# Operand sums of a second-level product: made by transfers inside DRAM instead of on the vector engine

## The chip, the core and the metric

The program runs on one core of a Trainium2 chip. The metric is the device time of one execution in microseconds; the kernel before takes 680.3 us (median of three runs, 679.74 to 681.45).

Engines are named as in the profile: PE is the tensor engine's matmul, PEld its weight load, DVE the vector engine, ACT the scalar engine, POOL the GpSimd engine, SP the sync engine. SP and POOL each issue transfers in their own program order. An instruction that has to wait holds up everything behind it on its engine.

## The reference

`x` is 2048 x 512, float32. The result mixes a Fourier transform and a gated two-layer network with a gate per row:

```
a = x @ dft_hid_re.T ; b = x @ dft_hid_im.T
A = dft_seq_re @ a - dft_seq_im @ b
B = (silu(x @ w1) * (x @ w3)) @ w2          # w1, w3: 512 x 1376
g = sigmoid((x * gate_w).sum(-1))
out = g * A + (1 - g) * B
```

## The kernel before

Every float32 product is made of three matmuls on a split operand: a high part (rounded, made by ACT at line 110) and a low part (the rest, made by DVE at line 113). `mm3` (line 126) issues the three. A matrix product over 2 x 2 blocks is done by a scheme with seven block products instead of eight, so each stage also needs sums of operand blocks; DVE makes those.

**First stage, gate and up projection.** Steps n = 1 to 21 (`gate_up`, line 333) each do seven products of six matmuls on PE. Beside them in a step DVE and ACT combine results (lines 356 to 394), prepare the next weight chunk (`sums_wb`, lines 246 to 249, then a split), and run work that tables attach to a step (`early`, `ahead`, `second`, `mid`, `at_end`, by step number). Line 369 adds PSUM bank `x` to a tile; the seventh product of the same step writes into that bank again, so it waits for line 369.

Three attached jobs matter here. First, steps 2 to 9 (lines 528 to 553) make four sums of quarters of the sequence matrix `cc`: eight 512 KB loads into SBUF on SP's queue (names `q0b`, `q1b`), eight subtractions of 128 x 1024 on DVE (line 546), eight 512 KB stores to a DRAM array `tsp` on POOL's queue (line 547). Their tiles come from the two `ZO` places. Second, four groups of `w2` are loaded, summed, split and stored to `w2sp` (lines 557 to 585), at the steps named in `W2_AT`; the split parts also take the two `ZO` places. Third, the transform's left operands are prepared at the steps in `A1_AT`.

**Second stage, the transform over the sequence.** Blocks 0 to 3 (`KIND` "F"), then two blocks of the down projection ("H") and two of the hidden transform ("Y"). A block is a list of steps; in block 0 a step is twelve matmuls. `step(m)` ends with `advance(m)` (line 762): it asks SP for loads of steps up to m + 8, lets DVE make the operand sum of step m + 4 (lines 730 and 734) and lets ACT and DVE split the operand of step m + 3 (tiles `zo`). `at(blk, n, f)` (line 1206) runs `f` just before step n of a block. In block 0 these are, among others, loads of the second half of the left operand (`load_a2`, tiles `xs`, steps 4 to 11), their subtraction on DVE (line 178, steps 7 to 14) and the gate (`gates`, steps 5 to 8, which ends with two stores on POOL).

**The second level.** Block 2's first product P1 is not done in block 2: it is itself split into seven quarter products m1 to m7, each in two halves "a" and "b", which are set between the steps of blocks 1 and 2 by the table `AMONG` (line 655). m1 uses B11 as it is; m5, m6, m7 and m4 use the quarter sums T1, T2, T3, T4 from `tsp`. m6 adds on to the PSUM bank of m1 after ACT has copied that bank (line 934). The left operands' sums S are made in `sums_s` (line 882).

Nothing reorders the work: each engine runs its instructions in the order in which the program text emits them, and waits on semaphores only for what it needs.

Of the kernel before, what the change touches and what calls it, by code (L numbers as in the profile page):

```python
# [7 lines left out]
F32 = mybir.dt.float32  # L8
F32R = mybir.dt.float32r
AF = mybir.ActivationFunctionType  # L10
ALU = mybir.AluOpType
# [14 lines left out]
LOOK = 3  # L26
K = 9
TAIL = 256
W2_AT = (10, 11, 13, 15)
A1_AT = (12, 14, 16, 17, 18, 19, 20)  # L30


# [1 line left out]
def fnet_swiglu_gate_kernel(  # L34
# [21 lines left out]
    nc = tc.nc  # L56
# [25 lines left out]
    def bank(k, name):  # L82
        return psum.tile([P, 512], F32, tag=f"ps{k}", name=name)
# [8 lines left out]
    def take(places, shape, dtype, name):  # L92
        p, tag = at = places.pop(0)
        t = p.tile(shape, dtype, tag=tag, name=name)
        HELD[id(t)] = t, places, at
        return t
# [4 lines left out]
    def parts(name):  # L101
        return take(ZO, [P, 2, 4, 256], F32R, name)

    def free(*tiles):
        for t in tiles:
            _, places, at = HELD.pop(id(t))
            places.append(at)
# [18 lines left out]
    def mm3(ps, ah, al, bh, bl, first, last, chain=False, some=slice(None)):  # L126
        for n, (u, v) in enumerate(((ah, bh), (ah, bl), (al, bh))):
            matmul(ps, u, v, some, start=first and n == 0, stop=last and n == 2,
                   skip_group_check=chain)
# [11 lines left out]
    tsp = dram.tile([4, 2, P, 1024], F32, tag="tsp", name="tsp")  # L141
# [185 lines left out]
    early, ahead, second, mid, at_end = {}, {}, {}, {}, {}  # L327
# [88 lines left out]
    b12, a21 = zt[0].rearrange("p h a n -> p h (a n)"), zt[1][:, :, 0]  # L416
# [91 lines left out]
    def do(work, n, f, *a):  # L508
        work.setdefault(n, []).append(lambda: f(*a))
# [15 lines left out]
    for n, k in ((7, "B12"), (7, "B11"), (8, "B21"), (9, "B22")):  # L525
        do(early, n, lambda k=k: free(ST[1, k]))

    BQ = {}

    def load_quarter(h, b, t):  # L530
        BQ[h, b] = t
        nc.sync.dma_start(t, cc[2 + (b[2] == "2"), 0, 2 * (b[1] == "2") + h])

    def load_quarters(h):
        for b in ("b11", "b12"), ("b21", "b22"):
            t = BQ[h, b] = parts(f"q{h}{b[0]}")
            v = t.bitcast(F32).rearrange("p h a n -> p h (a n)")
            for i in range(2):
                load_quarter(h, b[i], v[:, i])

    def sum_quarter(h, i):


        to, u, v = (("b11", "b12", "b11"), ("b22", "b22", "b11"),
                    ("b12", "b22", "b12"), ("b21", "b21", "b22"))[i - 1]
        nc.vector.tensor_sub(BQ[h, to], BQ[h, u], BQ[h, v])  # L546
        nc.gpsimd.dma_start(tsp[i - 1, h], BQ[h, to])

    for h, at_n in enumerate(((2, 3, 4, 4, 5), (5, 6, 7, 8, 9))):
        do(at_end, at_n[0], load_quarters, h)  # L550
        for n, i in zip(at_n[1:], (1, 3, 2, 4)):
            do(at_end, n, sum_quarter, h, i)
        do(at_end, at_n[4], lambda h=h: free(BQ[h, ("b11", "b12")], BQ[h, ("b21", "b22")]))

    W2R = {}

    def load_w2(p):
# [47 lines left out]
    for n in range(NI):  # L605
        if n in W2_AT:
            p = W2_AT.index(n)
            do(mid if p > 1 else at_end, n - 1, load_w2, p)
# [3 lines left out]
        if n in A1_AT:  # L612
            p = A1_AT.index(n)
# [9 lines left out]
    n = NI - 1 - LOOK  # L623
    do(at_end, n - 1, F4.extend, [(f4_a, f"f4_{k}") for k in range(4, 5 + LOOK)])
    for k in range(LOOK + 2):
# [26 lines left out]

    QUARTERS = {"m1": ("B11", 0, 0), "m2": ("B11", 0, 1), "m4": ("T4", 1, 1), "m5": ("T1",),
                "m6": ("T2",), "m7": ("T3",), "m3": ("B22",)}
    AMONG = {(1, 22): ("m1a",), (1, 23): ("m1b", "m6a"), (1, 24): ("m6b",), (1, 25): ("m7a",), (1, 26): ("m7b",),
             (1, 27): ("m4a", "m4b"), (2, 4): ("m2a",), (2, 5): ("m2b",), (2, 6): ("m5a",),
             (2, 7): ("m5b",), (2, 8): ("m3a",), (2, 9): ("m3b",)}
    STEPS, NEW, MAT = [], {}, {}
    for blk, nq in enumerate(NQ):
        todo_p1 = []  # L660
        for n, (k, form, q) in enumerate((k, form, q) for k, form in ORDER[blk] for q in range(nq)):
# [7 lines left out]
            STEPS.append((blk, q, k, form))  # L669
            for name in AMONG.get((blk, n), ()):  # L670
                k, h = name[:2], "ab".index(name[2])
# [90 lines left out]
    def advance(m):  # L762
        load_c(m + LEAD + AHEAD)
        sum_c(m + LEAD + 1)
        split_c(m + LEAD)
# [108 lines left out]
    SR, SF, MB = [], {}, {}  # L874
# [7 lines left out]
    def sums_s(j):  # L882
        (a11, a21), (a12, a22) = ((t[:, :, :P], t[:, :, P:]) for t in SR)
        if j == 0:
            nc.vector.tensor_add(a22, a21, a22)
            nc.vector.tensor_sub(a21, a11, a21)
        else:
            nc.vector.tensor_sub(a11, a22, a11)
            nc.vector.tensor_sub(a12, a12, a11)

    def high_s(i):
        SF[i] = [take(F4, [P, 1024], F32R, f"s{i}{k}") for k in "hl"[: 2 - i]]
# [7 lines left out]
    def quarter(k, h, i):  # L900

        kk = 2 * h + i
        if len(QUARTERS[k]) == 3:
            _, r, half = QUARTERS[k]
            w = A1[4 * half + kk][:, :, 1, r * P : (r + 1) * P]
            return w[:, 0], w[:, 1]
        t, at = {"m6": (0, 0), "m7": (0, P), "m3": (1, 0), "m5": (1, P)}[k]
        return [v.rearrange("p (k n) -> p k n", k=4)[:, kk, at : at + P] for v in SF[t]]

    def seeds(blk, *banks):  # L910
        U["P1"] = list(banks)
        new_banks("P2", blk)
        for r in range(2):
            nc.scalar.activation(U["P2"][r], banks[r], AF.Copy)

    def step_quarter(m):
        _, h, k, _ = STEPS[m]
        zt = ZT.pop(m)
        z = zt.rearrange("p h a n -> p h (a n)")
        to = {"m2": 4, "m5": 7, "m3": 6}.get(k, 5)  # L920
        own = k in ("m1", "m5")
        if own and h == 0:
            MB[to] = bank(to, f"quarter{to}")
        for i in range(2):
            b = slice(i * 512, (i + 1) * 512)
            mm3(MB[to], *quarter(k, h, i), z[:, 0, b], z[:, 1, b], own and h == i == 0, h == i == 1,
                not own)
        free(zt)
        advance(m)
        if h == 0:  # L930
            return
        if k == "m1":
            MB[4] = bank(4, "quarter4")
            nc.scalar.activation(MB[4], MB[5], AF.Copy)
        elif k == "m6":
            MB["u"] = ut.tile([P, 2, 512], F32, tag="u2", name="uu")
            nc.scalar.activation(MB["u"][:, 0], MB[5], AF.Copy)
        elif k == "m7":
            nc.scalar.activation(MB["u"][:, 1], MB[5], AF.Copy)
            free(*SF[0])  # L940
        elif k == "m2":
            seeds(2, MB[4], MB[5])
        elif k == "m5":
            MB[6] = bank(6, "quarter6")
            nc.vector.tensor_add(MB[6], MB[7], MB["u"][:, 0])
            nc.vector.tensor_add(MB[7], MB[7], MB["u"][:, 1])
        elif k == "m3":
            free(SF[1][0])

# [68 lines left out]
    def step(m):  # L1018
        blk, q, k, form = STEPS[m]
        if k[0] == "m":  # L1020
            return step_quarter(m)
# [184 lines left out]
    def at(blk, n, f, *a):  # L1206
        todo.setdefault(NEW[START[blk] + n], []).append((f, a))
# [10 lines left out]
    for g, n in enumerate((5, 3)):  # L1218
        for i in range(4):
            at(g, n + i, gates, g, i)  # L1220
    at(1, 12, load_s)
    for i in range(2):
        at(1, 15 + i, sums_s, i)
        at(1, (18, 24)[i], high_s, i)
        at(1, (20, 25)[i], low_s, i)
    LATES = (1, 10, "u3"), (2, 10, "u3"), (3, 10, "u3"), (3, 17, "s1"), (NTB + 1, 4, "s1")
    late = [(w2, w2sp, p) for p in range(len(W2_AT), NP2)] + [(dd, dsp, p) for p in range(KD)]
    for i, (src, sp, p) in enumerate(late):
        blk, n, tag = LATES[i]
# [105 lines left out]
```

## Time and profile before

| | |
|---|---|
| median of three runs | 680.3 us |
| the profiled execution | 679.96 us, span 677.8 us |
| granted clock of the tensor engine | 1.000 |
| PE busy | 667.7 us, 99% |
| DVE busy | 598.3 us, 88% |
| ACT busy | 378.0 us, 56% |
| POOL busy | 66.2 us, 10% |
| moved by DMA | 185.92 MB, 274 GB/s over the span |

The span runs from the first to the last instruction; 2.16 us of the profiled execution's time lie outside it. In a timeline a row gives the start, the length, the engine, the source line, the operation, the tiles written and read, how many were merged, and in brackets the idle time before it with what ended it. In a chain a row gives start, length and what it was. SPq and POOL rows that read DMA_DIRECT2D are the issues of transfers, not the transfers.

### The profile page before, as it was taken

To read this page: it belongs to the slowest core of one execution; us is meant where nothing else is said; L and a number is where in the kernel's file an instruction comes from. 1 tells how busy PE (TensorE), PEld (TensorE's weight loads), DVE (VectorE), ACT (ScalarE), POOL (GpSimd) and SP (SyncE) were. 2 spreads that over 40 slices of the span, in tenths; PEclk is the share of its full clock that TensorE was granted. 3 is DMA by queue.
4 is the path that set the end of the run, shared out by engine and by line. 5 is a ranking of instruction groups with operands and counts; after the bars stand their busy time and mean duration, and the time that the engine had idled before them with its cause. 6 is when DMAs were issued, how large, how long until landed. Compare 5 with 4: busy or idle time off the path is not lost.

```text
span 677.8 us, 8698 instructions
## 1 busy us (share of the span) xinstructions
PE 667.7 (99%) x3089; PEld 577.2 (85%) x3089; DVE 598.3 (88%) x707; ACT 378.0 (56%) x483; POOL 66.2 (10%) x122
## 2 busy tenths in 40 slices
PE   9999899999999999999999999999999999999997
PEld 6887688888888888888888888888888888888887
DVE  6978998787768999997999998999998699798896
ACT  5765455665546783566556564455546537546452
POOL 0012121221111000001000010001100011010000
PEclk9999999999999999999999999999999999999999
DMA  7697795599995975554849647727999969984942
GB/s 294 212 382 288 292 387 198 204 334 399 389 418 204 409 260 162 206 221 158 309 164 333 203 152 297 278 79 289 402 416 329 307 219 361 356 316 182 343 127 93
DMA packets 50811, 185.92 MB, mean 274 GB/s; under 512 B 5968, under 2 KB 7376, under 8 KB 47056
## 3 DMA queue, kind: packets, MB, share of 16 engines
q1 hardware_dynamic: 37024, 129.38, 53.8%
q0 software_dynamic: 13312, 55.33, 20.6%
q10 hardware_dynamic: 432, 0.66, 0.3%
q8 instruction: 24, 0.39, 0.2%
q14 instruction: 19, 0.16, 0.1%
HBM read 125.83 MB, written 59.51 MB: 273 GB/s over the span
## 4 chain that ended last, share of the span: by engine, by line
PE 84%; DVE 8%; DMA 4%; issue 2%; ACT 1%; SPq 0%; DVEq 0%; ACTq 0%; POOLq 0%
PE P L124 55%; PE quarter L124 12%; PE X L124 10%; PE Z L124 5%; DMA ws<-w 2%; PE Y L124 2%; DVE wa L113 1%; DVE xo L113 1%; DMA xs_B<-xt 1%; DVE xs_B L207 1%; DMA w2sp<-w2a 1%; DVE q0b L546 1%; DVE wu L247 1%; DVE wu L249 0%; DVE h L391 0%
## 5 line engine op out<-in xcount | busy, mean ns | idle before, releaser
L110 ACT ACTIVATE zo<-B 128x1024 fp32r<-128x1024 f32 x178 | 180.8, 1021 | 165.7 <-DVE B L730 65.3
L113 DVE TENSOR_TENSOR zo<-B,zo 128x1024 fp32r<-128x1024 f32 x178 | 208.3, 1178 | 22.6 <-ACT zo L110 21.6
L124 PE MATMUL P<-zo,a 128*128 128x512 f32 x960 | 209.7, 379 | 0.0
L124 PEld LDWEIGHTS P<-zo,a 128*128 128x128 f32 x960 | 181.4, 189 | 25.9
L124 PE MATMUL X<-xo,wb 128*128 128x512 f32 x378 | 89.2, 381 | 4.7 <-DVE u L369 4.7
L730 DVE TENSOR_TENSOR B<-B,B 128x1024 f32<-128x1024 f32 (+1 forms) x78 | 91.8, 1176 | 0.1
L124 PE MATMUL P<-zo,H 128*128 128x512 f32 x420 | 91.3, 379 | 0.0
L124 PEld LDWEIGHTS P<-zo,H 128*128 128x128 f32 x420 | 79.2, 189 | 11.8 <-issue 0.7
L124 PEld LDWEIGHTS X<-xo,wb 128*128 128x128 f32 x378 | 70.6, 189 | 16.9 <-DVE u L369 6.5
L124 PE MATMUL quarter<-zo,a 128*128 128x512 f32 x324 | 72.0, 379 | 0.0
L124 PE MATMUL P<-zo,Y 128*128 128x512 f32 (+1 forms) x336 | 71.6, 375 | 0.0
L124 PEld LDWEIGHTS P<-zo,Y 128*128 128x128 f32 x336 | 62.7, 189 | 8.7
L124 PEld LDWEIGHTS quarter<-zo,a 128*128 128x128 f32 x324 | 61.2, 189 | 8.7
L324 POOL DMA_DIRECT2D hsp<-h x40 | 21.9, 548 | 110.8 <-DVE h L375 65.8
L124 PE MATMUL X<-xo,wa 128*128 128x512 f32 x126 | 30.7, 381 | 0.4 <-ACT sc L310 0.4
L124 PE MATMUL Z<-xo,wa 128*128 128x512 f32 x126 | 30.7, 380 | 0.0
L124 PE MATMUL Z<-xo,wb 128*128 128x512 f32 x126 | 30.6, 379 | 0.0
L734 DVE TENSOR_TENSOR B<-B,B 128x1024 f32<-128x1024 f32 (+1 forms) x26 | 30.6, 1177 | 0.0
L124 PE MATMUL Y<-xo,wa 128*128 128x512 f32 x126 | 30.5, 379 | 0.0
L124 PEld LDWEIGHTS X<-xo,wa 128*128 128x128 f32 x126 | 23.6, 189 | 4.4 <-ACT sc L310 0.8
L113 DVE TENSOR_TENSOR wa<-ws,wa 128x768 fp32r<-128x768 f32 (+1 forms) x22 | 19.3, 880 | 9.1 <-ACT wa L110 9.1
L124 PEld LDWEIGHTS Z<-xo,wa 128*128 128x128 f32 x126 | 23.7, 189 | 3.6 <-ACT u L360 0.3
(185 smaller groups left out, 662.0 us busy)
## 6 DMA issues: line engine op xcount, KB each, us to landing
B<-cc SPq DMA_DIRECT2D x64, 512.0 KB, 5.7
hsp<-h POOLq DMA_DIRECT2D x40, 256.0 KB, 5.8
wbsp<-wb POOLq DMA_DIRECT2D x8, 1024.0 KB, 6.5
wb<-wbsp SPq DMA_DIRECT2D x8, 1024.0 KB, 8.3
B<-hsp SPq DMA_DIRECT2D x16, 512.0 KB, 8.2
B<-zsp SPq DMA_DIRECT2D x16, 512.0 KB, 8.1
ws<-w SPq DMA_DIRECT2D x11, 512.0 KB, 8.1
H<-w2sp SPq DMA_DIRECT2D x5, 1024.0 KB, 11.8
```

Of the source, the lines that this page charges most:

```text
L110: nc.scalar.activation(hi, src, AF.Copy)
L113: nc.vector.tensor_sub(lo, src, hi.bitcast(F32))
L124: nc.tensor.matmul(ps.rearrange("p (n a) -> p n a", a=2), u, turns(v)[:, some], **kw)
L207: nc.vector.tensor_sub(t, *(ST[g, v] for v in SUMS[k]))
L247: nc.vector.tensor_sub(u[:, 1], u[:, 0], r[:, 0])
L324: nc.gpsimd.dma_start(hsp[g, b + k, j // 2, :, j % 2 * 512 : (j % 2 + 1) * 512], h)
L546: nc.vector.tensor_sub(BQ[h, to], BQ[h, u], BQ[h, v])
L730: nc.vector.tensor_add(t, t, RAW[blk, b, q][:, :n])
L734: nc.vector.tensor_sub(t, RAW[blk, "B12", q][:, :n], t)
```

## The change

The quarter sums leave the first stage: the eight loads, eight subtractions and eight stores go. In block 0 of the second stage POOL issues eight transfers of 1 MB from DRAM to DRAM instead: for each of the four sums a plain copy into `tsp` and then a transfer that accumulates a second block on to it. T2 starts from a copy of T1, and T4 from a copy of T2. An accumulating transfer only adds, so the sums have plain signs now, and signs in `sums_s` and in the step after m5 turn to match. The first of the four `w2` groups moves from step 10 to step 9. In `AMONG` the second half of m1 comes directly after the first, so that a step of block 1 lies between m1 and m6.

```diff
-W2_AT = (10, 11, 13, 15)
+W2_AT = (9, 11, 13, 15)
...
-    def load_quarter(h, b, t):
-        BQ[h, b] = t
-        nc.sync.dma_start(t, cc[2 + (b[2] == "2"), 0, 2 * (b[1] == "2") + h])
...
-    def sum_quarter(h, i):
...
-        nc.vector.tensor_sub(BQ[h, to], BQ[h, u], BQ[h, v])
-        nc.gpsimd.dma_start(tsp[i - 1, h], BQ[h, to])
-
-    for h, at_n in enumerate(((2, 3, 4, 4, 5), (5, 6, 7, 8, 9))):
-        do(at_end, at_n[0], load_quarters, h)
-        for n, i in zip(at_n[1:], (1, 3, 2, 4)):
-            do(at_end, n, sum_quarter, h, i)
...
-    AMONG = {(1, 22): ("m1a",), (1, 23): ("m1b", "m6a"), (1, 24): ("m6b",), (1, 25): ("m7a",), (1, 26): ("m7b",),
+    AMONG = {(1, 22): ("m1a", "m1b"), (1, 23): ("m6a",), (1, 24): ("m6b",), (1, 25): ("m7a",), (1, 26): ("m7b",),
...
-            nc.vector.tensor_add(a22, a21, a22)
+            nc.vector.tensor_sub(a22, a21, a22)
...
-            nc.vector.tensor_sub(a12, a12, a11)
+            nc.vector.tensor_add(a12, a12, a11)
...
-            nc.vector.tensor_add(MB[6], MB[7], MB["u"][:, 0])
-            nc.vector.tensor_add(MB[7], MB[7], MB["u"][:, 1])
+            nc.vector.tensor_sub(MB[6], MB[7], MB["u"][:, 0])
+            nc.vector.tensor_sub(MB[7], MB[7], MB["u"][:, 1])
...
+    def quarter_sum(i, b, **kw):
+        src = tsp[int(b[1]) - 1] if b[0] == "T" else cc[2 + (b[2] == "2"), 0, 2 * (b[1] == "2") :][:2]
+        nc.gpsimd.dma_start(tsp[i - 1], src, max_dma_last_dim=4096, **kw)
+
+    for n, i, b, c in ((0, 1, "b12", "b11"), (1, 3, "b12", "b22"), (2, 2, "T1", "b22"),
+                       (3, 4, "T2", "b21")):
+        at(0, 3 + 7 * n, quarter_sum, i, b)
+        at(0, 6 + 7 * n, lambda i=i, c=c: quarter_sum(i, c, accum_op=ALU.add))
```

Where the instructions move. On DVE, between the end of step 4 and line 369 of step 5 of the first stage, before (`h` and `u` are results of a step, `xo` and `xs_B` the other operand's split and sums, `wu` the weight sums, `X` a PSUM bank):

```order
L391 TENSOR_TENSOR h_552<-h_552,u_4_553 128x512
L546 TENSOR_TENSOR q0b_468<-q0b_471,q0b_468 128x1024
L546 TENSOR_TENSOR q0b_471<-q0b_471,q0b_468 128x1024
L113 TENSOR_TENSOR xo_385<-xs_B_386,xo_385 128x1024
L207 TENSOR_TENSOR xs_B_386<-xs_B_392,xs_B_386 128x1024
L246 TENSOR_TENSOR wu_652<-ws_397 128x256
L247 TENSOR_TENSOR wu_652<-wu_652,ws_397 128x256
L248 TENSOR_TENSOR wu_652<-ws_397 128x256
L249 TENSOR_TENSOR wu_652<-ws_397,wu_652 128x256
L369 TENSOR_TENSOR u_5_633<-u_5_633,X_418 128x512
```

The same place with the change:

```order
L391 TENSOR_TENSOR h_544<-h_544,u_4_545 128x512
L113 TENSOR_TENSOR xo_385<-xs_B_386,xo_385 128x1024
L207 TENSOR_TENSOR xs_B_386<-xs_B_392,xs_B_386 128x1024
L246 TENSOR_TENSOR wu_640<-ws_397 128x256
L247 TENSOR_TENSOR wu_640<-wu_640,ws_397 128x256
L248 TENSOR_TENSOR wu_640<-ws_397 128x256
L249 TENSOR_TENSOR wu_640<-ws_397,wu_640 128x256
L369 TENSOR_TENSOR u_5_621<-u_5_621,X_418 128x512
```

The two quarter subtractions are gone and nothing takes their place. On POOL, from the last stores of the first stage (`hsp`) through block 0 (`gsp` and `ngsp` are the gate, `zsp` the block's results), before:

```order
L324 DMA hsp<-h_1786 128x512 x2
L324 DMA hsp<-h_1838 128x512 x2
L832 DMA gsp<-s1g_1927 128x1024
L833 DMA ngsp<-u2g_1928 128x1024
L960 DMA zsp<-zu_0_2182 128x1024
L960 DMA zsp<-zs_0_2426 128x1024
L960 DMA zsp<-zp_0_2085 128x1024
L960 DMA zsp<-zc_0_2485 128x1024
```

With the change:

```order
L324 DMA hsp<-h_1810 128x512 x2
L1198 DMA tsp<-cc 256x1024 x2
L805 DMA gsp<-s1g_1899 128x1024
L806 DMA ngsp<-u2g_1900 128x1024
L1198 DMA tsp<-cc 256x1024 x2
L1198 DMA tsp<-tsp 256x1024
L1198 DMA tsp<-cc 256x1024
L1198 DMA tsp<-tsp 256x1024
L933 DMA zsp<-zu_0_2157 128x1024
L933 DMA zsp<-zs_0_2405 128x1024
L933 DMA zsp<-zp_0_2059 128x1024
L1198 DMA tsp<-cc 256x1024
```

Two of the eight stand ahead of the gate's stores, five between these and the block's results, one before the last result; each pair is a copy and its accumulation, and the accumulation waits on POOL until the copy has landed. On PE in block 1, around m1 and m6 (`quarter` is their PSUM bank, `P` a step of block 1, `s0h` the high part of S), before:

```order
L124 MATMUL quarter_2938<-zo_2905,a_0_1233 128x512 x3
L124 MATMUL quarter_2938<-zo_2905,a_1_1392 128x512 x3
L124 MATMUL P_1_0_2565<-zo_2920,a_6_2226 128x512 x3
L124 MATMUL P_1_0_2565<-zo_2920,a_7_2245 128x512 x3
L124 MATMUL P_1_1_2566<-zo_2920,a_6_2226 128x512 x3
L124 MATMUL P_1_1_2566<-zo_2920,a_7_2245 128x512 x3
L124 MATMUL quarter_2938<-zo_2935,a_2_1549 128x512 x3
L124 MATMUL quarter_2938<-zo_2935,a_3_1621 128x512 x3
L124 MATMUL quarter_2938<-zo_2946,s0h 128x512 x2
```

With the change:

```order
L124 MATMUL quarter_2918<-zo_2885,a_0_1205 128x512 x3
L124 MATMUL quarter_2918<-zo_2885,a_1_1364 128x512 x3
L124 MATMUL quarter_2918<-zo_2900,a_2_1521 128x512 x3
L124 MATMUL quarter_2918<-zo_2900,a_3_1593 128x512 x3
L124 MATMUL P_1_0_2545<-zo_2915,a_6_2202 128x512 x3
L124 MATMUL P_1_0_2545<-zo_2915,a_7_2221 128x512 x3
L124 MATMUL P_1_1_2546<-zo_2915,a_6_2202 128x512 x3
L124 MATMUL P_1_1_2546<-zo_2915,a_7_2221 128x512 x3
L124 MATMUL quarter_2918<-zo_2926,s0h 128x512 x2
```

The twelve matmuls of a block 1 step now stand between the end of m1 and the start of m6. As line numbers of the change are 27 lower behind the removed functions, L1198, L805 and L933 there are the new transfers and the old L832 and L960.

More of the change, by code (lines that the diff above doesn't have):

```diff
@@ L526, in fnet_swiglu_gate_kernel @@
         do(early, n, lambda k=k: free(ST[1, k]))
-    BQ = {}
-    def load_quarter(h, b, t):
-        BQ[h, b] = t
[L532 to L539, printed above, removed]
-    def sum_quarter(h, i):
-        to, u, v = (("b11", "b12", "b11"), ("b22", "b22", "b11"),
-                    ("b12", "b22", "b12"), ("b21", "b21", "b22"))[i - 1]
-        nc.vector.tensor_sub(BQ[h, to], BQ[h, u], BQ[h, v])
-        nc.gpsimd.dma_start(tsp[i - 1, h], BQ[h, to])
-    for h, at_n in enumerate(((2, 3, 4, 4, 5), (5, 6, 7, 8, 9))):
-        do(at_end, at_n[0], load_quarters, h)
-        for n, i in zip(at_n[1:], (1, 3, 2, 4)):
-            do(at_end, n, sum_quarter, h, i)
-        do(at_end, at_n[4], lambda h=h: free(BQ[h, ("b11", "b12")], BQ[h, ("b21", "b22")]))
     W2R = {}
```

## The prediction

> **What bounds the kernel now.** First the page, its busy times.
>
> ```profile
> PE 667.7 (99%) x3089; PEld 577.2 (85%) x3089; DVE 598.3 (88%) x707; ACT 378.0 (56%) x483; POOL 66.2 (10%) x122
> ```
>
> PE is the bound: what can be gained is its idle time, about 10 us, part of it at the two ends. So next the waits of PE, and where each lies in its timeline.
>
> ```profile
> PE X L124 <- DVE u L369: 4.7, 4, 2.0
> PE quarter L124 <- ACT quarter L934: 0.7, 1, 0.7
> PE X L124 <- ACT sc L310: 0.4, 1, 0.4
> ```
> ```profile
> 60.71 2.88 PE L124 MATMUL X<-xo,wb 128*128 128x512 f32 x12 [1.03 <-DVE u L369]
> 72.11 2.88 PE L124 MATMUL X<-xo,wb 128*128 128x512 f32 x12 [2.04 <-DVE u L369]
> 82.13 2.88 PE L124 MATMUL X<-xo,wb 128*128 128x512 f32 x12 [0.66 <-DVE u L369]
> ...
> 100.47 2.75 PE L124 MATMUL X<-xo,wb 128*128 128x512 f32 x12
> ...
> 109.54 2.75 PE L124 MATMUL X<-xo,wb 128*128 128x512 f32 x12
> ...
> 132.15 1.56 PE L124 MATMUL X<-xo,wa 128*128 128x512 f32 x6 [0.44 <-ACT sc L310]
> ...
> 138.69 2.88 PE L124 MATMUL X<-xo,wb 128*128 128x512 f32 x12 [0.97 <-DVE u L369]
> ```
> ```profile
> 352.05 0.70 PE L124 MATMUL quarter<-zo,s0h 128*128 128x512 f32 x2 [0.67 <-ACT quarter L934]
> ```
>
> Six waits inside the program, 5.81 us together; an undisturbed step of the first stage takes 109.54 - 100.47 = 9.07 us. Behind 138.69 us there is one wait to the end, so whatever is gained early is kept unless a new wait appears.
>
> **The three waits from 60 to 82 us.** The timeline of DVE and the chain of waits:
>
> ```profile
> 53.62 0.96 DVE L113 TENSOR_TENSOR wa<-ws,wa 128x768 fp32r<-128x768 f32 x1 [2.34 <-ACT wa L110]
> ...
> 55.10 1.22 DVE L546 TENSOR_TENSOR q0b<-q0b 128x1024 f32<-128x1024 f32 x1
> ...
> 59.98 0.68 DVE L369 TENSOR_TENSOR u<-u,X 128x512 f32<-128x512 f32 x1
> ...
> 65.12 2.47 DVE L546 TENSOR_TENSOR q0b<-q0b,q0b 128x1024 f32<-128x1024 f32 x2
> ...
> 71.38 0.68 DVE L369 TENSOR_TENSOR u<-u,X 128x512 f32<-128x512 f32 x1
> ...
> 81.39 0.68 DVE L369 TENSOR_TENSOR u<-u,X 128x512 f32<-128x512 f32 x1
> ```
> ```profile
> 37.44 15.22 DMA ws<-w
> ```
> ```profile
> 31.25 2.16 SPq L532 DMA_DIRECT2D q0b<-cc  x4
> ```
>
> From one line 369 to the next DVE needs 71.38 - 59.98 = 11.40 us and then 10.01 us, against PE's 9.07. Without the subtractions, two in the first of these steps and one in the second, they are 11.40 - 2.47 = 8.93 and 10.01 - 1.22 = 8.79: DVE keeps up. The first wait, 1.03, has two causes ahead of it: 1.22 of subtraction, and 2.34 of idling for a `ws` load that took 15.22 us because four `q0b` loads (2.1 MB) stood ahead of it in SP's queue. The stretch moved 351 GB/s (row below), so without them the load lands 2.1 / 0.351 = 6.0 us earlier, at 46.7 us, ahead of the 51.3 at which DVE began to idle. DVE is then 3.6 us earlier, 2.5 us ahead of need. Taken: all 3.73 us go.
>
> **The two waits at 132 and 138 us.**
>
> ```profile
> 129.12 0.42 ACT L110 ACTIVATE w2a<-w2r 128x256 fp32r<-128x256 f32 x1 [4.50 <-DMA w2sp<-w2a]
> ```
> ```profile
> 123.72 5.34 DMA w2sp<-w2a
> ...
> 134.36 0.96 DVE w2b L113
> ```
> ```profile
> 130.26 1.46 PE L124 MATMUL Z<-xo,wb 128*128 128x512 f32 x6
> ```
> ```profile
> 132.62 0.59 ACT L356 ACTIVATE h<-X 128x512 f32<-128x512 f32 x1
> 133.48 0.84 ACT L110 ACTIVATE w2b<-w2r 128x768 fp32r<-128x768 f32 x1 [0.27 <-ACT h L356]
> ```
>
> ACT idles 4.50 us: the second `w2` group wants the place `w2a` that the first group's store still reads. With the first group a step, 9.07 us, earlier that store goes out that much earlier and has landed before ACT asks. What remains is the chain of step 12: when the step's first product is done, at 130.26, ACT reads it (0.59) and splits `w2b` (0.84), and DVE's low part begins at 131.7 at the earliest instead of 134.36. From there to PE's start at 138.69 it took 4.33 us, so PE can go on at 136.0, and without its own two waits it gets there at 138.69 - 0.97 - 0.44 = 137.3. That is 1.3 us to spare, which ACT's other operations in between (0.6 us each) can use up; I leave 0.2 of the 1.41.
>
> Moved with the group are one load on SP (now ahead of two `ws` loads), seven operations on DVE, three on ACT and two stores on POOL (now ahead of step 10's `hsp` pair). They fall in a stretch, 82 to 132 us, in which PE had no wait even with the `q1b` subtractions, which now are gone; that is their cover, and without it up to the store's 5.34 us would be paid again.
>
> **The wait at 352 us.** Before, m6 follows m1 at once and waits for ACT's copy; now a step of twelve matmuls (2.59 us, below) covers the 0.59 of it.
>
> ```profile
> 351.41 0.59 ACT quarter L934
> ```
> ```profile
> 342.69 3.49 DVE L113 TENSOR_TENSOR zo<-B,zo 128x1024 fp32r<-128x1024 f32 x3
> ```
>
> m1b runs 2.59 us sooner. Its split is one of three that DVE makes in a row; as the second it ends at 345.0, and PE gets there at 347.3. Its load moves past one other on SP. So 0.67 goes. Signs cost nothing: the same operations, adding for subtracting.
>
> **The eight new transfers.** Nothing makes POOL wait for the step to which they are attached: the first copy depends on no earlier work of the block, so it goes out right behind the last `hsp` store, its accumulation when it has landed, and the other three pairs behind the gate's stores.
>
> ```profile
> 215.85 0.55 POOL L324 DMA_DIRECT2D hsp<-h  x1 [0.15 <-issue]
> 237.40 0.54 POOL L832 DMA_DIRECT2D gsp<-s1g  x1 [21.00 <-ACT s1g L831]
> ```
> ```profile
> 30.00:60.00 30.00, 29.68 (x138) 25.60 (x136) 23.52 (x38) 15.77 (x23) 5.41 (x10) 1.00 0.92 351
> ...
> 219.50:240.50 21.00, 21.00 (x99) 18.37 (x99) 20.72 (x22) 15.79 (x20) 1.07 (x2) 1.00 1.00 398
> 240.50:260.00 19.50, 19.50 (x92) 17.09 (x91) 19.40 (x23) 13.77 (x16) 0.00 (x0) 1.00 0.56 193
> ```
>
> The last two columns are the DMA share and GB/s. The first pair lands in the worst place: 21 us with all DMA engines busy (1.00, 398 GB/s). One pass of 1 MB at that rate is 2.6 us, by which loads behind it come later; the other pairs fall where half is free. Who is hurt? DVE, which there has no idle time, and through it PE:
>
> ```profile
> 234.67 0.42 DVE L178 TENSOR_TENSOR xs<-xs 128x256 f32<-128x256 f32 x1
> ...
> 236.14 1.22 DVE L113 TENSOR_TENSOR zo<-B,zo 128x1024 fp32r<-128x1024 f32 x1
> 237.28 0.41 DVE L178 TENSOR_TENSOR xs<-xs 128x256 f32<-128x256 f32 x1
> 237.97 1.23 DVE L113 TENSOR_TENSOR zo<-B,zo 128x1024 fp32r<-128x1024 f32 x1 [0.28 <-ACT zo L110]
> ```
> ```profile
> 218.68 7.47 SPq L791 DMA_DIRECT2D xs<-xn  x5
> ```
> ```profile
> DMA to landing us min/median/max: 12.8/13.1/13.4
> ```
> ```profile
> 214.09 132.10 PE P L124 x612
> ```
>
> The first two `xs` loads took 12.8 and 13.4 us and landed at 231.5 and (issued at 219.3) 232.7; DVE read them at 234.67 and 237.28: slack 3.2 and 4.6. A block 0 step is 12 of those 612 matmuls, 2.59 us, so step k begins at 214.09 + 2.59 k. The split at 236.14 is for step 10 (240.0) and ends at 237.4: 2.6 us ahead of PE; the next one ends at 239.2, 3.4 ahead of step 11 at 242.6. So a load must come 3.2 + 2.6 = 5.8 us later (the second 8.0) before PE waits.
>
> What a copy and an accumulation cost in DMA time no row shows. Below: one pass each, 5.3 us together, no wait of PE. Above: each as two transfers, a read and a write, 10.5 us, hence 4.7 us of wait. I take one pass for the copy, since the old transfers' other side in SBUF cost no pass of its own, and two for the accumulation, which reads two blocks where a copy reads one: 7.9 us. The second load then comes 7.9 later, just within 8.0. The first can be delayed by the copy's 2.6 and by that part of the accumulation that has run when it comes; as the accumulation cannot start before the copy has landed, the middle of 2.6 and 7.9, 5.3, would cost nothing and the full 7.9 would cost 2.1. I take 0.6. Below nothing is not in reach here, as PE has no wait in block 0 to lose. An issue takes POOL 0.55 us for 128 rows, at most twice that for 256, and holds nobody: its next urgent work is the gate's store at 237.40, which waits for ACT.
>
> The Trainium skill, "Collectives: The Full Stack", section "The bandwidth ceiling: the fold count and why AG ≠ RS ≠ AR", speaks against the change here: an add in a transfer needs two source reads on one ring, and ran at half a copy's rate. By that the accumulation is the 5.3 us taken, by one pass the 0.6 would be nothing. No trace so far shows it.
>
> **The sum.** Profiled execution 679.96 - 3.73 - 1.21 - 0.67 + 0.60 = 674.95. The median of the runs shown is 0.34 above the profiled execution: 675.3 us.
>
> **Rivals.**
>
> 1. *The accumulation holds the DMA engines far longer than two passes.* Place: the first pair, 216 to 240 us, with the later ones behind it. With A us for one accumulation the second `xs` load comes 2.6 + A later and PE waits 2.6 + A - 8.0. That eats the 5.0 us gained from A = 10.4, four passes. At five passes, 13.2, it is 7.8 us, and the later pairs, which then overlap the loads behind 241 us as well, add some 2: 674.35 + 7.8 + 2 + 0.34 = 684.5, slower. For it: DVE has no idle time there, and no row shows an adding transfer. Against: a pass of 2.6 us would have to be stretched fivefold.
> 2. *Block 0 takes part of the gain.* Two passes for every new transfer, 4.7 us of wait as worked out, or the pairs behind 238 us meeting the last `xs` loads: 677 to 679.4. For it: 1.00 DMA share. Against: only the loads of some 10 us are tight.
> 3. *A new wait follows the old in the first stage.* DVE at 8.93 of 9.07 us a step has no reserve; a late ACT or load would leave half of the 4.9 us: 677.7. For it: the 0.2 at step 12. Against: from 82 us on, with the `q1b` subtractions still there, PE did not wait until 132.
>
> **How the numbers follow.** My forecast 0.61, rival 1 0.08, rival 2 0.17, rival 3 0.14. A measurement of this kernel can tell about 0.3%, 2.0 us, from no change. Faster (under 678.3): forecast, rival 3 nearly whole, half of rival 2: 0.81. Within: the rest of 2, a little of 3 and of 1: 0.12. Slower: 0.07. The forecast's own range is 673.9 (the lowest run, 679.74, less all 5.81) to 676.5; the range to 679.5 takes in the upper bound of block 0.
>
> **What would show it.** Right: PE's list without L369 and without the copy of the quarter bank; DVE from one line 369 to the next near 9.1 us; ACT without the 4.5 us idle; the first copy issued at once behind the last `hsp`, and PE without a wait of over 1 us in block 0. Wrong on block 0: DVE idle before line 178 or 730 near 225 to 240 us, and PE waiting for `zo`. Wrong as a whole: an accumulation that takes over 10 us to land and a PE wait behind it as large as the gain.

## The result, and the profile after

The changed kernel takes 675.6 us (median of six runs, 674.43 to 676.72), the kernel before 680.8 us (six runs beside them, 679.39 to 681.68). The ratio is 0.9925, with a 95% interval from 0.9908 to 0.9942: 5.2 us faster. The forecast was 675.3 us. Its total is right, but its gains and its cost are each about 2 us too small and offset one another; the experiments below show both.

The profiled execution after took 674.43 us with a span of 672.6 (before 679.96 and 677.8). From its page, the busy times; and from the waits of PE, every row of 0.3 us or more behind the start of the program:

```profile
PE 666.4 (99%) x3089; PEld 577.8 (86%) x3089; DVE 589.7 (88%) x699; ACT 377.3 (56%) x483; POOL 68.2 (10%) x122
```
```profile
PE P L124 <- ACT zu L1048: 1.1, 1, 1.1
...
PE P L124 <- DVE zo L113: 0.7, 2, 0.5
```

Nothing is left of line 369, of `sc` or of the quarter bank; in their place stand two new entries, both in the transform. PE's timeline shows where: the row of 612 matmuls (block 0 and most of block 1) is now broken three times.

```profile
206.62 44.67 PE L124 MATMUL P<-zo,a 128*128 128x512 f32 x205
251.58 18.18 PE L124 MATMUL P<-zo,a 128*128 128x512 f32 x83 [0.28 <-DVE zo L113]
270.87 26.38 PE L124 MATMUL P<-zo,a 128*128 128x512 f32 x121 [1.11 <-ACT zu L1048]
297.71 44.08 PE L124 MATMUL P<-zo,a 128*128 128x512 f32 x203 [0.46 <-DVE zo L113]
```

**What a wait really costs.** Block 0 now begins at 206.62 us, before at 213.93: 7.31 us earlier, where the five waits of the first stage that went were listed with 5.14. Some 0.65 of the difference is the start of the program (the first `wb` step begins at 23.90 us, before at 24.55, and nothing of the change is ahead of it). The rest is in how a wait is listed. Two rows of the kernel before beside the prediction's row at 72.11, and one of its page:

```profile
68.61 1.46 PE L124 MATMUL Y<-xo,wa 128*128 128x512 f32 x6
...
74.83 1.46 PE L124 MATMUL Z<-xo,wb 128*128 128x512 f32 x6
```
```profile
L124 PE MATMUL P<-zo,a 128*128 128x512 f32 x960 | 209.7, 379 | 0.0
```

In the profile a matmul takes 379 ns from start to end, but in an undisturbed stretch the next starts 216 ns after it (2.59 us for 12). From 68.61 six matmuls should take 1.30; the next row starts 3.50 later: 2.21 lost, not the 2.04 listed, since idle time is counted only from the end of the last matmul, 0.16 us after the next could have begun. The twelve matmuls after the wait then need 2.72 in place of 2.59: another 0.13. So each of these waits costs about 0.3 us more than its listed time. I count "lost" in this way from here on, from start to start:

| us lost by PE | before | after |
|---|---|---|
| start of the program, to 24 us | 1.41 | 0.78 |
| first stage | 6.78 | 0.11 |
| blocks 0 and 1, without m1 and m6 | 0 | 0.71 + 1.38 + 0.72 = 2.81 |
| m1 and m6 | 0.93 | 0 |
| behind that | 0.23 | 0.36 |
| sum | 9.35 | 4.06 |

The difference, 5.29 us, agrees with that of the spans, 5.2.

**The first stage.** DVE's line 369 now comes in PE's step and waits for PE itself, where before PE waited for it:

```profile
56.55 0.69 DVE L369 TENSOR_TENSOR u<-u,X 128x512 f32<-128x512 f32 x1 [0.19 <-PE X L124]
...
74.68 0.69 DVE L369 TENSOR_TENSOR u<-u,X 128x512 f32<-128x512 f32 x1 [0.19 <-PE X L124]
```

The two are 18.13 us apart, two steps of PE's 9.07. The `ws` load that took 15.22 us takes 6.4.

**Block 0.** POOL's timeline for the new transfers, and DVE's for the subtraction of the eight `xs` loads:

```profile
209.17 0.58 POOL L1198 DMA_DIRECT2D tsp<-cc  x1
...
222.73 0.95 POOL L1198 DMA_DIRECT2D tsp<-cc  x1 [12.98 <-DMA tsp<-cc]
...
235.75 0.58 POOL L1198 DMA_DIRECT2D tsp<-cc  x1 [4.45 <-issue]
```
```profile
227.46 0.42 DVE L178 TENSOR_TENSOR xs<-xs 128x256 f32<-128x256 f32 x1
...
230.06 0.42 DVE L178 TENSOR_TENSOR xs<-xs 128x256 f32<-128x256 f32 x1
...
233.63 0.42 DVE L178 TENSOR_TENSOR xs<-xs 128x256 f32<-128x256 f32 x1 [0.78 <-DMA xs<-xn]
...
236.44 0.42 DVE L178 TENSOR_TENSOR xs<-xs 128x256 f32<-128x256 f32 x1 [0.38 <-DMA xs<-xn]
...
239.04 0.43 DVE L178 TENSOR_TENSOR xs<-xs 128x256 f32<-128x256 f32 x1 [0.18 <-DMA xs<-xn]
...
243.79 0.42 DVE L178 TENSOR_TENSOR xs<-xs 128x256 f32<-128x256 f32 x1 [2.32 <-DMA xs<-xn]
...
246.82 0.43 DVE L178 TENSOR_TENSOR xs<-xs 128x256 f32<-128x256 f32 x1 [0.60 <-DMA xs<-xn]
...
249.97 0.43 DVE L178 TENSOR_TENSOR xs<-xs 128x256 f32<-128x256 f32 x1 [0.71 <-DMA xs<-xn]
```

The first two loads arrive in time. The third to the eighth do not: DVE idles 4.97 us before them in all, by 250 us the splits' lead is used up, and PE waits at 251.58. The table has, for each load, the slack in the kernel before (from its landing to DVE's read of it), and how much later, counted from the start of block 0, it lands now:

| `xs` load | 1 | 2 | 3 | 4 | 5 | 6 | 7 | 8 |
|---|---|---|---|---|---|---|---|---|
| slack before, us | 3.2 | 4.6 | 6.0 | 7.1 | 8.1 | 7.9 | 4.7 | 2.5 |
| lands later by, us | 2.6 | 4.1 | 6.9 | 8.5 | 9.8 | 12.0 | 9.2 | 7.9 |

Of this delay, 2.2 to 3.6 us of the last four loads is that SP issues them later; the seventh, for one, is issued when the gate's first store lands. DVE then runs without a pause to catch up, so ACT, which splits what DVE has summed, reaches its copy of P1 (line 1048) late, and the step that wants the bank waits at 270.87. The third wait has its own cause, in the chain of waits of the kernel after:

```profile
261.53 12.36 DMA tsp<-cc
...
277.72 7.95 DMA zsp<-zs
285.71 8.60 DMA s1g<-gs
...
296.43 1.24 DVE zo L113
297.71 2.43 PE P L124 x10
```

The `zsp` store, beside T4's transfers, takes 7.95 us (before 2.89); the load of the gate into the same tile waits for it, ACT waits for that load, and the split behind it in ACT's order is late.

### The profile page after: what moved, and what is told of

Its sections match the earlier page's. It is cut to its first block, busy times and chain, and to the rows that moved or that the text cites. A ratio compares the mean times of both kernels' runs of the same rounds, so it can differ in the third digit from the quotient of the medians.

```text
span 672.6 us, 8661 instructions
## 1 busy us (share of the span) xinstructions
PE 666.4 (99%) x3089; PEld 577.8 (86%) x3089; DVE 589.7 (88%) x699; ACT 377.3 (56%) x483; POOL 68.2 (10%) x122
## 4 chain that ended last, share of the span: by engine, by line
PE 85%; DMA 7%; issue 4%; DVE 3%; ACT 1%; POOL 1%; SPq 0%; ACTq 0%; DVEq 0%; POOLq 0%
PE P L124 43%; PE X L124 16%; PE quarter L124 12%; PE Z L124 8%; PE Y L124 4%; DMA tsp<-tsp 2%; DMA tsp<-cc 2%; PE C L124 2%; DVE zo L113 1%; DMA s1g<-gs 1%; DMA zsp<-zs 1%; DVE B L703 1%; DMA xs_B<-xt 1%; ACT zo L110 0%; PE V L124 0%
## 5 line engine op out<-in xcount | busy, mean ns | idle before, releaser
L386 ACT ACTIVATE h<-X 128x512 f32<-128x512 f32 x21 | 12.5, 596 | 35.3 <-PE X L124 35.3
L124 PEld LDWEIGHTS Y<-xo,wa 128*128 128x128 f32 x126 | 23.8, 189 | 3.4
L124 PEld LDWEIGHTS Z<-xo,wb 128*128 128x128 f32 x126 | 23.8, 189 | 3.4
```

The source lines that it names most:

```text
L124: nc.tensor.matmul(ps.rearrange("p (n a) -> p n a", a=2), u, turns(v)[:, some], **kw)
L386: nc.scalar.activation(g1, x, AF.Silu)
```

## The experiments

All ran beside the kernel before, whose median in the three groups was 680.9, 680.7 and 680.6 us.

**Block 0 without the transfers.** The quarter sums are left out, and the second level reads one quarter of the sequence matrix in place of every sum.

```diff
-            return cc[3, 0, 2 + q] if k == "m3" else tsp[int(QUARTERS[k][0][1]) - 1, q]
+            return cc[3, 0, 2 + q]
...
-        at(0, 3 + 7 * n, quarter_sum, i, b)
-        at(0, 6 + 7 * n, lambda i=i, c=c: quarter_sum(i, c, accum_op=ALU.add))
```

> The changed kernel without its eight transfers: the quarter sums are left out, the seven-product part reads one quarter of the sequence matrix in place of every sum. The matmuls, the loads and the work of DVE and ACT are the same. In the changed kernel PE waits three times in blocks 0 and 1 (0.28, 1.11 and 0.46 us listed; counted from start to start of the matmuls 0.71 + 1.38 + 0.72 = 2.8 us lost). Theory: all three come from the transfers; without them the list of PE's waits has no zo and no zu, the span falls by 2.8 us to about 669.8, the time from 675.6 to about 672.8. Rival, the term of the prediction: block 0 costs 0.6, so the time is about 675.0 and waits of some 2 us stay. Second rival: block 0 begins 7.3 us earlier than before while its loads are no faster, so the wait for zu (1.38 lost) stays without any transfer: about 674.2.

Measured: 673.1 us (671.48 to 673.89), ratio 0.9882 (0.9851 to 0.9914), 2.5 us under the changed kernel. In PE's timeline blocks 0 and 1 are one row without a break:

```profile
206.94 123.42 PE L124 MATMUL P<-zo,a 128*128 128x512 f32 x571
```

So all three waits come from the transfers, and block 0 costs 2.8 us, not 0.6. Both rivals fall. The span is 672.1, not the 669.8 expected: 2.1 us of new waits appear at 560 to 580 us, in the down projection. They lie over 250 us behind the place of the transfers: two of them, 1.3 us, are taken up at the end; the third, 0.9 us at 581 us, ends a wait for a `B<-hsp` load of 8.5 us and was not followed further.

**Copies in place of the accumulations.** The additions are left out: each sum holds its second block alone.

```diff
-        at(0, 6 + 7 * n, lambda i=i, c=c: quarter_sum(i, c, accum_op=ALU.add))
+        at(0, 6 + 7 * n, lambda i=i, c=c: quarter_sum(i, c))
```

> The changed kernel with its four accumulating transfers made plain copies (so the additions are left out: the sums hold the second block alone). Same places, same bytes written. Theory: an accumulation takes the DMA engines two passes and a copy one, so about 4 x 2.6 = 10 us of DMA time go, the xs loads of block 0 come earlier and most of the 2.8 us that PE loses in blocks 0 and 1 goes: lost 0 to 1.2 us, time 672.8 to 674.0; a plain copy in the accumulation's place lands in about 8 us where the accumulation took 10.3 to 12.7. Rival: what hurts is that there are eight more transfers in that stretch at all, each sharing the engines with the loads; then PE loses 2 us or more and the time stays at 675 to 676.

Measured: 672.7 us (672.3 to 673.55), ratio 0.9881 (0.9851 to 0.9912). In blocks 0 and 1 PE loses 0.84 us, in one wait of 0.66 for `zu`; 2.0 us of the 2.8 are gone, so what hurts is mainly the accumulations' extra time and not that there are eight transfers. The four copies in the accumulations' places land in 5.4 to 12.4 us (expected about 8), the accumulations in 10.3 to 12.7. What the extra time is, the view of the DMA queues shows. First the changed kernel while T2's accumulation runs (261.5 to 273.9 us), then this one while the copy in its place runs (256.5 to 262.0); the columns are packets, MB, share of 16 engines, and in the last row the us to landing (12.36 for the accumulation, in the chain above):

```profile
q0 software_dynamic: 272, 1.05, 48.1%
```
```profile
q0 software_dynamic: 272, 1.05, 54.0%
...
tsp<-cc POOLq DMA_DIRECT2D x1, 1024.0 KB, 5.4
```

POOL's queue (q0) carries nothing but this transfer in either. The accumulation takes 0.481 x 12.4 x 16 = 95 us of single engines, 0.35 us a packet, the copy 0.540 x 5.5 x 16 = 48, 0.17 us a packet: 2.0 times, as the prediction took it; all engines together are held 6.0 us by the one and 3.0 by the other. The Trainium skill, "Collectives: The Full Stack", section "The bandwidth ceiling: the fold count and why AG ≠ RS ≠ AR", has the reduce-scatter of a collective, whose add needs two source reads, at half the rate of the all-gather's plain copy. It speaks of collectives between cores; the 2.0 of these rows, inside one core's DRAM, agrees with it.

The same in the first pair's place, changed kernel at 222.7 to 235.4 us, then copies at 222.9 to 232.4; the rows give the busy share in tenths and the GB/s, in 40 slices:

```profile
DMA  9999999999999999999999999998999999998999
GB/s 439 413 413 413 413 413 439 413 413 426 413 413 426 374 271 245 323 258 245 310 232 284 284 258 284 245 297 258 258 284 271 245 310 232 284 284 297 400 413 413
```
```profile
GB/s 431 414 414 448 397 431 397 448 379 466 379 500 328 500 328 500 345 483 380 466 397 431 397 414 431 414 431 397 431 397 500 345 483 345 483 362 483 345 483 362
```

While the accumulation moves, the engines stay busy at 9 tenths or more but carry some 270 GB/s where the copies carry 420. So at a full share it is the fall of GB/s that tells an accumulation from a copy.

The same view shows how this reaches the `xs` loads, which are on SP's queue (q1). In the changed kernel, from 213 to 220 us, while T1's copy moves, q0 has 368 packets and 50% of the engines, q1 383 packets and 51%. From 227 to 234 us, while T1's accumulation moves, q0 has 243 packets and 71%, q1 249 packets and 35%. Both queues get about as many packets, and those of an accumulation take twice as long; so beside a copy the loads had half of the engines, beside an accumulation a third.

**Where the transfers stand: T1's pair in the first stage, and all four there.** The sums are whole in both. First T1's pair:

```diff
+    for i, b, n, c, k in ((1, "b12", 8, "b11", 10),):
+        do(at_end, n, quarter_sum, i, b)
+        do(at_end, k, lambda i=i, c=c: quarter_sum(i, c, accum_op=ALU.add))
...
-    for n, i, b, c in ((0, 1, "b12", "b11"), (1, 3, "b12", "b22"), (2, 2, "T1", "b22"),
+    for n, i, b, c in ((1, 3, "b12", "b22"), (2, 2, "T1", "b22"),
```

> The changed kernel with the first pair (copy and accumulation of T1) moved into the first stage, behind its steps 8 and 10 (about 85 to 115 us, DMA share there 0.6); the other three pairs stay. Theory as the prediction has it, the first pair is the one in the worst place: DVE's idling before line 178 (5.0 us in all) goes but for some tenths, with it the waits of PE at 251 and 271 us (2.1 us lost); the wait at 298 us (0.72 lost) stays; about 673.5. Rival: the second pair, whose copy goes out with the gate's stores at 231 us and meets the last five xs loads, is as bad: DVE still idles 2 us or more there and PE still loses over 2 us in all: 675 or more.

Measured: 672.2 us (671.34 to 672.77), ratio 0.9872 (0.9841 to 0.9902). PE loses nothing in blocks 0 and 1, and DVE never idles for `xs`:

```profile
206.62 123.63 PE L124 MATMUL P<-zo,a 128*128 128x512 f32 x572
```

That is more than the theory said, as the wait at 298 us is gone too. The other pairs did not stay where they were: the first of them (T3) now goes out at 231 us behind the gate's stores, 22 us after the last `hsp` store, when five of the eight `xs` loads are in and the sixth is about to land (231.7).

Then all four:

```diff
+    for i, b, n, c, k in ((1, "b12", 2, "b11", 4), (3, "b12", 5, "b22", 7),
+                          (2, "T1", 8, "b22", 10), (4, "T2", 11, "b21", 13)):
+        do(at_end, n, quarter_sum, i, b)
+        do(at_end, k, lambda i=i, c=c: quarter_sum(i, c, accum_op=ALU.add))
```

> All eight transfers in the first stage, behind steps 2 and 4 (T1), 5 and 7 (T3), 8 and 10 (T2), 11 and 13 (T4); nothing of them is left in block 0. Theory: DMA share in the first stage between 24 and 140 us is about 0.6; four copies of 2.6 and four accumulations of 5.3 us add 31.6 us in 116, to about 0.9, which the ws loads stand: block 0 and 1 as without the transfers, no new wait: about 672.8. Rival: DVE has 8.9 of 9.07 us of work in a step there and the ws loads (6.4 us in the changed kernel, 15.2 before) grow again, so that PE waits for DVE's line 369 as before: each such wait 0.9 to 2.3 us, time 674 to 678.

Measured: 680.2 us (677.93 to 681.55), ratio 0.9986 (0.9969 to 1.0002): by the median the whole gain is gone. The profiled execution is the lowest of the twelve, 677.93 us, at a granted clock of 1.000; the other eleven had 0.995 to 0.997, and no trace shows what the 2.2 us from it to the median are. In it blocks 0 and 1 have no wait, as the theory said, but PE loses 6.1 us in the first stage, 3.4 of it in a wait for line 369 at 144 us. So the rival holds, though not for the stretch it named. Two windows (24 to 127 us and 127 to 165 us; the last two columns are DMA share and GB/s), the changed kernel first, then this one:

```profile
24.00:127.00 103.00, 103.00 (x479) 90.20 (x478) 84.58 (x129) 62.61 (x95) 17.54 (x32) 1.00 0.62 229
127.00:165.00 38.00, 38.00 (x178) 32.98 (x177) 30.73 (x50) 22.86 (x36) 8.33 (x15) 1.00 0.96 356
```
```profile
24.00:127.00 103.00, 103.00 (x479) 90.20 (x478) 84.67 (x128) 62.61 (x95) 21.98 (x38) 1.00 0.88 292
127.00:165.00 38.00, 34.34 (x159) 29.33 (x158) 26.36 (x43) 18.01 (x28) 8.58 (x15) 1.00 0.95 329
```
```profile
131.73 10.62 DMA w2r<-w
...
143.64 0.69 DVE u L369
...
144.38 1.78 PE X L124 x7
```

Six transfers ran in the first window, where the share rose from 0.62 to 0.88 and PE lost nothing (103.00 busy of 103.00). The second window was full already, 0.96, and T4's pair fell into it. The last fence is the chain of waits there: a `w2r` load of 10.6 us (in the changed kernel 7.4), issued while T4's copy and two `w2sp` stores behind it ran; DVE stands still for it with line 369 behind it. The other 2.7 us are three waits between 163 and 172 us, just behind T4's accumulation (148.3 to 162.0 us); the chain of the last of them goes back to an `xr` load of 14.9 us. The mean that I had gone by, 0.6 from 24 to 140 us, hid that the engines are full from 127 us on.

**Three pairs in the first stage, T4's in block 0.** This tells T4's pair from the other six transfers.

```diff
+    for i, b, n, c, k in ((1, "b12", 2, "b11", 4), (3, "b12", 5, "b22", 7),
+                          (2, "T1", 8, "b22", 10)):
...
+    at(0, 24, quarter_sum, 4, "T2")
+    at(0, 27, lambda: quarter_sum(4, "b21", accum_op=ALU.add))
```

> T1's, T3's and T2's pairs in the first stage at the steps of the run with all four there (2 and 4, 5 and 7, 8 and 10), T4's pair in block 0 as in the changed kernel. Theory: in the run with all four the stall at 140 us came from T4's pair alone, whose copy and the two w2sp stores held behind it met a w2r load (10.62 us, DVE idle 4.86); the six transfers before it fell in a stretch with room. So: no wait of PE in the first stage, none above 0.3 us in blocks 0 and 1, time 672 to 673. Rival: the first stage has no room for three pairs either, DVE's u (line 369) falls behind at steps 5 to 10 and PE waits there 1 us or more: 674 or more.

Measured: 672.7 us (672.1 to 673.57), ratio 0.9882 (0.9861 to 0.9902), nothing lost in the first stage nor in blocks 0 and 1, with the same share in the first window:

```profile
24.00:127.00 103.00, 103.00 (x478) 90.18 (x478) 84.57 (x128) 62.51 (x95) 22.13 (x38) 1.00 0.88 291
```

So the stall needs T4's pair; the other six transfers cost nothing here. Whether T4's pair would stall it without them was not tried.

**Is T1's pair the bad one?** The mirror image: T3's pair moved into the first stage, T1's left.

```diff
+    for i, b, n, c, k in ((3, "b12", 8, "b22", 10),):
...
-    for n, i, b, c in ((0, 1, "b12", "b11"), (1, 3, "b12", "b22"), (2, 2, "T1", "b22"),
+    for n, i, b, c in ((0, 1, "b12", "b11"), (2, 2, "T1", "b22"),
```

> The changed kernel with the second pair (T3) in the first stage behind steps 8 and 10, and T1's, T2's and T4's in block 0 as in the changed kernel; the mirror of the run with T1's pair moved, which lost nothing in blocks 0 and 1. Theory A, the prediction's: the first pair alone is in the worst place, so with it left there PE keeps the 2.1 us lost at 251 and 271 us: 674.9 or more. Theory B: what hurts is two pairs one behind the other over all eight xs loads (DVE idled 0.78, 0.38, 0.18 before the third to fifth, 2.32, 0.60, 0.71 before the sixth to eighth); with either one away the split's lead of some 3 us absorbs the rest: lost under 0.8 us in blocks 0 and 1, 672.5 to 674.

Measured: 675.6 us (674.74 to 676.66), ratio 0.9932 (0.9914 to 0.9949), no better than the changed kernel. From PE's timeline:

```profile
206.83 39.24 PE L124 MATMUL P<-zo,a 128*128 128x512 f32 x181
246.42 2.86 PE L124 MATMUL P<-zo,a 128*128 128x512 f32 x12 [0.36 <-DVE zo L113]
249.64 2.86 PE L124 MATMUL P<-zo,a 128*128 128x512 f32 x12 [0.36 <-DVE zo L113]
252.78 18.18 PE L124 MATMUL P<-zo,a 128*128 128x512 f32 x83 [0.28 <-DVE zo L113]
272.06 58.11 PE L124 MATMUL P<-zo,a 128*128 128x512 f32 x268 [1.11 <-ACT zu L1058]
```

Lost: 0.52 + 0.63 + 0.55 + 1.37 = 3.07 us. That is what theory A said, but the run doesn't tell A from B as I had meant it to: nothing holds POOL, so T2's copy moved up into T3's place (issued at 236.9 us, in the changed kernel T3's at 235.75), and again two pairs ran over the eight `xs` loads. What is shown by the two runs together is that three pairs of which the first is issued at 209 us, with the next one at its heels, cost some 3 us, and that three pairs of the same size starting at 231 us cost nothing. What the first pair would cost with nothing behind it was not tried, but the changed kernel's trace tells some of it. The third load landed at 233.6 us, before T3's copy was issued at 235.75, so DVE's 0.78 us of idling for it is not T3's. The sixth landed at 243.77, 8.0 us after that issue; as the two queues share the engines about evenly there (53% and 48% from 239.5 to 243.8 us), T3's copy can account for at most 4 of its 12.0 us (an estimate).

**T4's pair in block 1.**

```diff
-                       (3, 4, "T2", "b21")):
...
+    at(1, 7, quarter_sum, 4, "T2")
+    at(1, 9, lambda: quarter_sum(4, "b21", accum_op=ALU.add))
```

> The changed kernel with T4's pair in block 1, steps 7 and 9, behind the second gate's stores (about 302 us) in place of 274 to 294 us. Theory: the wait at 298 us (0.46 listed, 0.72 lost) comes from T4's transfers, which slow the zsp store and the s1g load behind it, so that ACT idles 5.44 us and the split is late; with them away it goes, the waits at 251 and 271 us stay. Rival: the zsp store and the s1g load collide with the block 1 loads anyhow, and a wait of 0.3 us or more is left at 298.

Measured in one run: 675.5 us. The wait at 298 us is gone, the two at 252 and 271 stay (0.85 and 1.38 lost): the theory holds. The time doesn't show it, as this execution lost 1.3 us in the down projection.

**The three small moves.** The kernel before without its quarter sums (as in the first experiment), and the changed kernel with either of its two table edits undone:

```diff
-W2_AT = (9, 11, 13, 15)
+W2_AT = (10, 11, 13, 15)
```
```diff
-    AMONG = {(1, 22): ("m1a", "m1b"), (1, 23): ("m6a",),
+    AMONG = {(1, 22): ("m1a",), (1, 23): ("m1b", "m6a"),
```

> The kernel before with its quarter sums left out (no loads, subtractions and stores of them; the seven-product part reads one quarter of the sequence matrix in place of every sum); W2_AT and AMONG as before. Theory: the three waits for line 369 at 60.71, 72.11 and 82.13 us go. By the prediction's term this is 3.73 us; counted from start to start of the matmuls it is 1.33 + 2.34 + 0.94 = 4.6 us, as every wait costs some 0.3 us beyond the listed idle time. So the first matmul of block 0 starts at 213.93 - 4.6 = 209.3 (by the listed times alone 210.2), apart from the start of the program, and the waits at 132, 138 and 352 us stay: time 676 to 677. Rival: without the sums the second w2 group's stall at 129 us goes too, as DVE and POOL have more room: 674 to 675, PE's list without sc L310 and without line 369.

> The changed kernel with the first w2 group back at step 10. Theory: ACT's stall for the place that the first group's store still reads comes back, and the two waits of PE in step 12, 0.44 and 0.97 us listed, 2.1 lost from start to start: block 0 starts 2.1 us later (208.7). Rival, by the prediction's 0.2 left and DVE's larger lead without the quarter sums: under 0.5 us.

> The changed kernel with m1's second half back beside m6. Theory: PE waits 0.67 us for ACT's copy of the quarter bank, 0.93 lost from start to start, and nothing else changes. Rival: the copy is earlier now, no wait over 0.2 us.

Measured: 676.2 us (674.64 to 676.96; ratio 0.9931, 0.9905 to 0.9956) without the sums; 676.5 and 677.0 in one run each for the two others, for which the waits count and not these times. From PE's waits, in this order:

```profile
PE X L124 <- DVE u L368: 1.0, 1, 1.0
...
PE quarter L124 <- ACT quarter L906: 0.7, 1, 0.7
...
PE X L124 <- ACT sc L309: 0.6, 1, 0.6
```
```profile
PE X L124 <- DVE u L369: 1.0, 1, 1.0
...
PE X L124 <- ACT sc L310: 0.6, 1, 0.6
```
```profile
PE quarter L124 <- ACT quarter L907: 0.7, 1, 0.7
```

Without the sums the three waits from 60 to 82 us are gone (block 0 begins at 208.87, expected 209.3 by the start-to-start count and 210.2 by the listed times), and the waits of step 12 and of m6 stay. With the `w2` group back, the two waits of step 12 return: 2.26 us lost, block 0 at 209.42. With m1 back, 0.94 us. So each of the three parts of the change removes its own waits, and neither of the others would have done it.

**A version that beats both.** T1's pair in the first stage once more, beside the changed kernel:

> The changed kernel once more, beside the variants of the same call: 675 to 676 us.

> The version with T1's pair in the first stage once more, in the same call as the changed kernel. Theory: it saves what PE loses in blocks 0 and 1, 2.8 us, so 672.2 to 673, and beats the changed kernel by 0.3 to 0.5%. Rival: the two differ by the run only, under 0.15% (1 us).

Measured: the changed kernel 676.7 us (674.63 to 678.77), ratio 0.9936 (0.9911 to 0.9961), above the 675 to 676 expected (in this trace PE loses 3.4 us in blocks 0 and 1, not 2.8, and 1.5 in the down projection); with T1's pair early 673.0 us (672.6 to 673.32), ratio 0.9885 (0.9866 to 0.9904). The two ratios lie 0.5% apart and their intervals don't meet: about 3.5 us faster than the changed kernel, and 7.6 faster than before.

## Why the prediction was right, and where it was not

- **The three waits from 60 to 82 us.** All went, by the causes named: line 369 comes every 9.07 us, `ws` lands in 6.4 us. The term, 3.73, was mis-sized: it added listed idle times, and start to start they were 1.33 + 2.34 + 0.94 = 4.61.
- **The two at 132 and 138 us.** They went wholly; the 0.2 that I left for ACT's other operations was not needed. But "1.3 us to spare" was too much: in step 12 line 369 now ends at 131.18 us, and the product of PE that waits for it starts at 131.39, so 0.2 was to spare. Listed 1.41, really 2.08. Undoing this edit brought 2.26 back.
- **The wait at 352 us.** Listed 0.67, really 0.93; undoing it brought 0.94.
- **Block 0.** The step that failed. The durations that I took were about right: a copy one pass, an accumulation two, 7.9 us for the pair, where 3.0 + 6.0 is measured. But I priced the delay on the first two `xs` loads alone, because their slack is the smallest among the six issued early, and had them carry what had run by then. The first two were indeed hit least, 2.6 and 4.1 us, and were in time. The later loads met the full accumulation, then the gate's stores, and from 235.75 us the second pair: the sixth came 12.0 us late, against 7.9 of slack. The last two I did not look at, and the eighth had the smallest slack of all, 2.5 us, and came 7.9 late. "The other pairs fall where half is free" was read off windows of the kernel before, in which the work that the first pair pushes back had not yet been pushed into them. In the changed kernel the window from 237 to 256 us has a full share:

```profile
237.00:256.00 19.00, 18.71 (x86) 15.76 (x85) 15.19 (x18) 11.12 (x14) 1.50 (x2) 1.00 1.04 366
```

- So block 0 cost 2.81 us, not 0.60. That is in part the mechanism of rival 2 ("the pairs behind 238 us meeting the last `xs` loads"), to which I gave 0.17; the third load was late by the first pair alone. Rival 2's times, 677 to 679.4, stand for 2.3 to 4.7 us of cost beside my other terms, and the 2.81 is inside; the time came out lower, as the gains were larger.
- **The sum.** With the measured terms: 679.96 - 4.61 - 2.08 - 0.93 + 2.81 = 675.15. The rest to 674.43 is the start of the program (0.63) and tenths elsewhere. That the predicted 674.95 came so close was luck: gains 2.0 us too small met a cost 2.2 us too small.
- **The other rivals.** Accumulations of four or five passes: no, two. A new wait in the first stage: none. The first copy went out at once behind the last `hsp` store, and POOL stood waiting 12.98 us for it, holding nobody, as said. "PE without a wait of over 1 us in block 0" failed by the one of 1.11, and the sign named for a wrong block 0 (DVE idle before line 178) is what the trace shows. All accumulating transfers here were issued with `accum_op=ALU.add`; whether one could subtract was not tried, so "only adds", in the description of the change, is not shown.

## What to carry to other kernels

Price a wait from the start of one row to the start of the next, not by its listed idle time: here each was worth 0.3 us more. Transfers added to busy DMA engines here delayed all eight loads that ran beside and behind them, the first by 2.6 us and the sixth by 12.0; so compare the delay with the slack of every later load, and expect a transfer that nothing holds to go out as early as its queue allows, not at the step in whose place it was written. Look for the place in windows of some 20 us rather than in a stage's mean: six transfers between 24 and 127 us cost nothing, and with two more behind 127 us PE lost 6.1 us.

## What was not expected of the hardware

Half of the 14 traces have waits of PE between 559 and 569 us, 1.1 to 1.5 us lost, in kernels that are the same there, and even in one of two profiled executions of the changed kernel. What differs with them is the order in which two engines issue, some 0.1 to 1.4 us apart. From the timelines of SP and POOL, first the execution without the waits, then the one with them, and of the latter its chain of waits:

```profile
550.35 0.73 POOL L934 DMA_DIRECT2D nbsp<-zc  x1 [4.49 <-DVE zc L931]
```
```profile
551.43 1.61 SPq L985 DMA_DIRECT2D Y<-dsp  x2
```
```profile
551.61 0.90 SPq L985 DMA_DIRECT2D Y<-dsp  x2
```
```profile
551.74 9.55 DMA nbsp<-zc
```

Where POOL's store of `zc` is issued ahead of SP's `Y` loads, by 0.8 to 1.4 us, it lands in 4.7 to 6.8 us (seven traces); where the first of these is ahead of it, by 0.1 to 0.5 us, in 9.2 to 9.6 us (the other seven), and then DVE, which wants its tile, is late and PE waits. The 14 hold no exception, but no run set the order on purpose, so that the order is the cause is not shown. That the runs of one kernel differ by some 2 us may come from this in part; that is not shown either.
